# One core: the order of SyncE's loads in a chunked recurrent attention, and the pace of a background substitution

## The chip, the cores and the metric

The kernel runs on one core of a Trainium2 chip. The metric is the device time of that core in microseconds, the median of the runs. A core has five engines, each with its own queue that is worked in order: TensorE (PE in the rows; its weight loads are PEld), VectorE (DVE), ScalarE (ACT), GpSimd (POOL) and SyncE (SP), which here does nothing but issue transfers. Where an instruction at the head of a queue waits, everything behind it on that engine waits too.

## The reference

A recurrent attention over B = 4 batches, H = 8 heads, S = 768 tokens and D = 40, followed by two feed-forward layers.

```
for t in range(S):
    y[:, :, t] = einsum('bhd,bhde->bhe', r_t, state)
    Sa    = einsum('bhde,bhe->bhd', state, a_t)
    state = state * w_t[:, :, None, :] - einsum('bhd,bhe->bhde', Sa, b_t) + einsum('bhd,bhe->bhde', v_t, k_t)
x   = y as [B, S, H*D]
h   = relu(x @ w_in);  x2 = (h * sigmoid(conv3(h, conv_w))) @ w_out
u,v = halves of relu(x2 @ w_in2);  out = (u * (w_spatial @ normalized(v) + b_spatial)) @ w_out2
```

The change touches the attention alone.

## The kernel before

**Tiling.** The tokens are cut into 6 blocks n of 128 (two chunks of 64 each). A *unit* is one batch of one block with its 8 heads, so there are 24 units, kk = 4n + i. Two batches of a block are a *pair* p = kk // 2; their rows are loaded together. Within a chunk the recurrence is solved by a triangular system: a matrix is built from a and b (generator A), its 32x32 diagonal parts are inverted by a substitution (subst), the inverse is put together (Bp), applied along the chain of states (Cp), and the output y is formed (Dp).

**The loop.** Unit kk of the main loop interleaves, in 19 *parts* z = 0 to 18, the generators of several units by the string ORDER = "CDCBDCBCAAZAZBAZABZ": A of unit kk+9, Bp of unit kk+1, Cp of unit kk, Dp of kk (letter Z, its first four steps) and of kk-1 (letter D, its last two). So part 3 of a unit is the first step of Bp(kk+1): the matmuls pf (L226), which read DT; part 6 is its second: px (L238), which reads D1. Part 5 is pu of the second chunk (L290), which reads VM, made by VectorE behind part 2 (L303, L305). Parts 1 and 4 finish y of the unit before; part 4 ends with the product of py and ln on VectorE (L348). Part 9 is the first of A's transposes of P (L164), which reads P after VectorE's product P*il (L142, "pm", step 4 of an odd unit).

**What is issued when.** After each part, in this order: what is due by the counter of parts (`later(m, f)` puts f off by m parts, `tick` counts), then `pump` with so many steps of the background work as the rate gives (RATE steps a part from unit 3 on, RATE0 before), then the entries of SCHED and SCHEDC for this part. All of it is program order: every engine works its queue in just this sequence, SyncE too.

**SyncE's queue.** In an even unit SCHED[0] gives, for the pair po = kk // 2 + 5: il (2 transfers, L131), P (4, L112), araw (1, L100), lnA (1, L105). il is multiplied into P; G (L118, GpSimd, part 18) is araw times lnA, and AR (L123) its copy. The store of x (L350) is put off by 2 parts from part 4. `loadD` (L211, L213: DT, and D1 in two transfers) is put off by DTL parts from px of an odd Bp; it loads the inverse for the next pair into the only buffers of DT and D1, which must have been read: DT by pf and by copies into bdN (L232, VectorE and GpSimd), D1 by px. At part 18 the matrix is stored (tb, L178, 4 transfers). In an odd unit SyncE loads ln (part 5) and four transfers of Z and UR (L266, part 6).

**Substitution.** When both pairs of block n have passed through A (units 2, 6, 10, 14), the block's matrices are loaded (L, L186) in part 6 of the unit after, and SUB parts later subst(n) is put into the background list. For n >= 2 a step is VectorE's addition (L193) of one j and GpSimd's product tmp (L191) of the next, each reading what the other wrote; 30 of them and a last one in which GpSimd copies LT (L196). DDL parts after the last step the inverse is stored (dt, L198, and dd, L199); `loadD` reads it back from there.

Of the kernel before, what the change touches and what calls it, by code (L numbers as in the profile page):

```python
# [11 lines left out]
def attention(tc, keep, ident, r,k,v,w,a,b, x, spare=None):  # L12
# [3 lines left out]
    sy=nc.sync; V=nc.vector; T=nc.tensor; G_=nc.gpsimd; AC=nc.scalar  # L16
    with ExitStack() as ctx:
# [64 lines left out]
        def later(m,f):  # L82
            due.append((now[0]+m,f)); 
# [98 lines left out]
        def subst(n,ps=slice(0,128)):  # L182
            np_=ps.stop-ps.start
            if n not in Ls: Ls[n]=(sb.tile([128,HB,HB],F32,name="L"),sb.tile([128,HB*HB//4],F32,name="tmp"),sb.tile([128,HB,HB],F32,name="LT"))
            L,tmp,LT=(t[ps] for t in Ls[n])
            BQ[0].dma_start(out=L,in_=tb_d[n][ps])  # L186
            yield
            for j in range(1,HB-1):
                m=HB-1-j
                t=tmp[:,0:m*j].rearrange("p (m k) -> p m k",m=m)  # L190
                (G_ if n>=2 else V).tensor_tensor(t,L[:,j+1:HB,j:j+1].to_broadcast([np_,m,j]),L[:,j:j+1,0:j].to_broadcast([np_,m,j]),ALU.mult)  # L191
                yield
                V.tensor_tensor(L[:,j+1:HB,0:j],L[:,j+1:HB,0:j],t,ALU.add)  # L193
                if n<2: yield
            V.memset(L.rearrange("p t j -> p (t j)")[:,0:HB*HB:HB+1],1.0)
            (V if n==0 else G_).tensor_copy(LT,L.rearrange("p t j -> p j t"))  # L196
            def put():
                BQ[0].dma_start(out=dt_d[n][ps],in_=LT)  # L198
                BQ[0].dma_start(out=dd_d[n],in_=Ls[n][0][0:128:2])  # L199
                stored.update((n,j) for j in range(2) if ps.start<=j*64<ps.stop)  # L200
            later(DDL,put)
            yield
        inv={}; stored=set()
        def loadD(p):

            if p>=NK//2: return
            n,j=p//2,p%2
            assert (n,j) in stored,(p,stored,now,due)
            DT=sb.tile([128,H2,HB],F32,name="DT",bufs=1); D1=sb.tile([96,H2,HB],F32,name="D1",bufs=1)
            hs=slice(j*H2*4,(j+1)*H2*4)  # L210
            BQ[0].dma_start(out=DT,in_=dt_d[n][hs].rearrange("(b h q) t j -> (q t) (b h) j",b=2,q=4))  # L211
            for c in range(2):
                BQ[0].dma_start(out=D1[c*C:c*C+HB],in_=dd_d[n][j*H2*2:(j+1)*H2*2].rearrange("(b h q) t j -> q t (b h) j",b=2,q=2)[c])  # L213
            inv[n,j]=(DT,D1)
        def Bp(kk):

            i,n=units[kk]
            u=st[kk]; G=pair[n,i//2]['G']; h0=(i%2)*H
            DT,D1=inv[n,i//2]
            N=bdN[0]  # L220
            F=sb.tile([96,H,HB],F32,name="F",bufs=1)
            pf=ps.tile([128,H,HB],F32,tag="ps",name="pf")
            for h in range(H):
                for c in range(2):
                    lo=slice(c*C,c*C+HB); hi=slice(c*C+HB,c*C+C)
                    T.matmul(pf[lo,h],lhsT=G[hi,h0+h,0:HB],rhs=DT[hi,h0+h],start=True,stop=True)  # L226
            for c in range(2):
                lo=slice(c*C,c*C+HB)
                AC.copy(F[lo],pf[lo])
            for q in range(4):  # L230
                qs=slice(q*HB,(q+1)*HB)
                (G_.tensor_copy if q%2 else V.tensor_copy)(N[qs,:,q*HB:(q+1)*HB],DT[qs,h0:h0+H])  # L232
            yield
            px=ps.tile([128,H,HB],F32,tag="ps",name="px")
            for h in range(H):
                for c in range(2):
                    lo=slice(c*C,c*C+HB)
                    T.matmul(px[lo,h],lhsT=D1[lo,h0+h],rhs=F[lo,h],start=True,stop=True)  # L238
            for c in range(2):
                lo=slice(c*C,c*C+HB)  # L240
                AC.copy(N[lo,:,c*C+HB:c*C+C],px[lo])
            if i%2==1: later(DTL,lambda: loadD(kk//2+1))
            yield
            WT=u['WT']=[]
            for g in range(2):
                W=sb.tile([104,4,128],F32,name="WT",bufs=4); WT.append(W)
                p=ps.tile([128,4,128],F32,tag="ps",name="pw")
                for j in range(4):
                    T.matmul(p[:104,j],lhsT=G[:,h0+g*4+j,C:],rhs=N[:,g*4+j],start=True,stop=True)  # L249
                AC.mul(W,p[:104],-1.0)  # L250
                yield
# [55 lines left out]
        def Dp(kk):  # L307

            i,n=units[kk]
            pr=pair[n,i//2]; P=pr['P']; UR=pr['UR']; VM=st.pop(kk)['VM']; h0=(i%2)*H; bs=slice(i//2*2,i//2*2+2)  # L310
            s0=n*128
            ln,y=pr['ln'],pr['y']
            py=None
            ZVs,bdRs,SSs={},{},{}
            for part,g in ("z0","z1","S0","S1","y0","y1"):
                g=int(g)
                if part=="z":

                    ZV=ZVs[g]=sb.tile([80,4,168],F32,name="ZV",bufs=2)
                    bdR=bdRs[g]=sb.tile([80,4,2,C],F32,name="bdR",bufs=2)  # L320
                    p=ps.tile([128,4,2,C],F32,tag="ps",name="pz")
                    for j in range(4):
                        T.transpose(p[:80,j].rearrange("p c t -> p (c t)"),UR[:,h0+g*4+j].rearrange("p c e -> p (c e)"),ident)
                    AC.copy(ZV[:,:,0:C],p[:80,:,0])
                    for c in range(2):
                        AC.activation(bdR[:,:,c],p[:80,:,1],AF.Copy,scale=mB[:,c:c+1])
                    p=ps.tile([128,4,104],F32,tag="ps",name="pv")
                    for j in range(4):
                        T.transpose(p[:80,j],VM[:,g*4+j].rearrange("p c d -> p (c d)"),ident[:104,:104])
                    AC.copy(ZV[:,:,C:],p[:80])  # L330
                elif part=="S":
                    ZV,bdR=ZVs[g],bdRs[g]
                    SS=SSs[g]=sb.tile([128,4,2,C],F32,name="SS",bufs=2)
                    p=ps.tile([128,4,2,C],F32,tag="ps",name="pS")
                    for j in range(4):
                        T.matmul(p[:,j].rearrange("p c t -> p (c t)"),lhsT=ZV[:,j,0:2*C],rhs=bdR[:,j].rearrange("p c t -> p (c t)"),start=True,stop=True)  # L336
                    V.tensor_tensor(SS.rearrange("p h c t -> p (h c) t"),p.rearrange("p h c t -> p (h c) t"),mS.unsqueeze(1).to_broadcast([128,8,C]),ALU.mult)  # L337
                else:
                    ZV,bdR,SS=ZVs[g],bdRs[g],SSs[g]
                    if py is None: py=ps.tile([128,H,D],F32,tag="ps",name="py")  # L340
                    for j in range(4):
                        h=g*4+j
                        for c in range(2):
                            T.matmul(py[c*C:(c+1)*C,h],lhsT=SS[:,j,c],rhs=P[:,h0+h,c],start=True,stop=False)  # L344
                        for c in range(2):
                            T.matmul(py[c*C:(c+1)*C,h],lhsT=bdR[:,j,c],rhs=ZV[:,j,2*C:],start=False,stop=True)  # L346
                    if g==1:
                        V.tensor_tensor(y[:,h0:h0+H],py,ln[:,h0:h0+H],ALU.mult)  # L348
                        if i%2==1:
                            later(2,lambda: (AC if kk==NK-1 else sy).dma_start(out=x[bs,s0:s0+128].rearrange("b t f -> t b f"),in_=y.rearrange("p (b h) e -> p b (h e)",b=2)))  # L350
                yield

        units=[(i,n) for n in range(NU) for i in range(B)]
        NK=len(units)
# [17 lines left out]
        with tc.manual_schedule(engines={mybir.EngineType.SP,mybir.EngineType.DVE}):  # L372
            flat=lambda t: t.rearrange("p h e -> p (h e)")[:,0:512]
            def both(g,f):

                for _ in g:
                    yield
                    next(f,None)
            def steps(g,m):
                for _ in range(m): next(g,None)  # L380
# [22 lines left out]
            s0=subst(0); next(s0)  # L403
# [7 lines left out]
            s0=both(s0,chain((0 for _ in range(OFF)),l4))  # L411
            at=0
            for z in range(2):
                g=A(4+z); steps(g,3)
# [28 lines left out]
            with tc.manual_schedule():  # L443
# [9 lines left out]
                for kk in range(NK):  # L453
                    i,n=units[kk]
# [6 lines left out]
                    for g in ORDER if kk<TAIL else ORDER2:  # L461
# [5 lines left out]
                        while done<ex(kk-1)+(ex(kk)-ex(kk-1))*(z+1)//19:  # L467
                            next(later_layer,None); done+=1
                        tick(); acc+=RATE0 if kk<3 else RATE; pump(int(acc)); acc-=int(acc)
                        for s,f in SCHED[(kk+LA+1)%2]+SCHEDC[kk%2]:  # L470
                            if s==z:
# [21 lines left out]
OFF=24  # L493
L4N=21
L4T=15
RATE=0.65
RATE0=1.4
SCHED=[[[1, "il"], [5, "P"], [6, "araw"], [7, "ln"], [18, "g"], [18, "ar"]], [[1, "dup"], [4, "pm"]]]
SCHEDC=[[[2, "V"], [6, "Z"]], [[5, "Y"], [6, "Z"], [10, "V"]]]
SUB=4  # L500
TBL=3
LL2=7
LL=7
DDL=5
DTL=7
PMV=1
WARM0=3
WARM1=2
# [506 lines left out]
```

## Time and profile before

| | us |
|---|---|
| median of 3 runs (1005.5 to 1006.63) | 1005.76 |
| the profiled execution | 1006.02 |
| its span, first to last instruction | 1004.3 |
| TensorE busy | 861.1 (86%) |
| VectorE busy | 644.9 (64%) |
| ScalarE busy | 501.1 (50%) |
| GpSimd busy | 294.2 (29%) |
| mean granted TensorE clock | 0.895 |

The attention takes the span up to about 530 us, the loop over the units from about 123 us; the layers take the rest. Busy time of TensorE is counted at the clock that was granted: a stretch at half clock is busy and slow at once, so the share of busy time hides what a wait costs behind it. A unit of the loop is read best from the start of its pf. Where a row ends in brackets, these are the idle time of the engine just before and what ended it.

### The profile page before, as it was taken

The numbers are of one execution on the slowest core, as the hardware profiler recorded it, in microseconds if no ns is written. First come the engines' busy times: TensorE is split into PE (matmuls) and PEld (weight loads), VectorE is DVE, ScalarE is ACT, GpSimd is POOL, SyncE is SP. The second block draws the span as 40 slices with busy tenths as digits, with TensorE's granted clock in tenths as the row PEclk, the third lists the DMA queues.
The fourth block names the chain that finished last, engine by engine and source line by source line (L and its number), as shares of the span: only waits on it lengthen the run. The fifth ranks groups of instructions, "written<-read, shape, count | busy, mean of one in ns | idle before, by whom it ended". The sixth has DMA issues, their size and how long they took to land. (4 is left out here: it accounts for less than half of the span.)

```text
span 1004.3 us, 22325 instructions
## 1 busy us (share of the span) xinstructions
PE 861.1 (86%) x8923; PEld 806.9 (80%) x8923; DVE 644.9 (64%) x1412; ACT 501.1 (50%) x1115; POOL 294.2 (29%) x413
## 2 busy tenths in 40 slices
PE   0528579799989889979979789998999989998997
PEld 0326479788879889879868679998999979998897
DVE  6399688365464465577576997548763787258841
ACT  0423346456456555546765565346542665256531
POOL 1112021263262362453330001224412342234311
PEclk9965588798789789767978989999999999999999
DMA  7999898975785683646441132111000110011001
GB/s 131 199 192 189 153 191 126 161 111 106 130 132 111 104 133 86 148 76 147 101 125 56 64 93 75 38 47 54 1 24 20 52 42 24 21 40 31 10 1 44
DMA packets 292065, 90.04 MB, mean 90 GB/s; under 512 B 270960, under 2 KB 285040, under 8 KB 290800
## 3 DMA queue, kind: packets, MB, share of 16 engines
q1 hardware_dynamic: 291680, 88.20, 44.0%
q8 instruction: 72, 1.18, 0.5%
q14 instruction: 41, 0.34, 0.1%
q10 hardware_dynamic: 272, 0.33, 0.1%
HBM read 64.91 MB, written 23.59 MB: 88 GB/s over the span
## 5 line engine op out<-in xcount | busy, mean ns | idle before, releaser
L665 PE MATMUL psp<-spt,vv 128*128 128x384 f32 x576 | 105.5, 338 | 0.5 <-DVE vv L793 0.3
L665 PE MATMUL ph<-XT,G 128*128 128x386 f32 x512 | 103.2, 348 | 0.9 <-DVE XT L698 0.9
L665 PEld LDWEIGHTS psp<-spt,vv 128*128 128x128 f32 x576 | 100.2, 188 | 2.2 <-ACT vv L790 1.0
L193 DVE TENSOR_TENSOR L<-L,tmp 128x30 f32<-128x30 f32 (+9 forms) x180 | 67.1, 373 | 51.1 <-POOL tmp L191 49.1
L665 PEld LDWEIGHTS ph<-XT,G 128*128 128x128 f32 x512 | 94.4, 195 | 1.5 <-DVE XT L698 1.1
L727 POOL TENSOR_TENSOR gl<-c,gh 128x384 fp32r<-128x384 f32 x48 | 66.2, 1378 | 89.8 <-ACT gh L725 75.4
L191 POOL TENSOR_TENSOR tmp<-L 128x30 f32<-128x30 f32 (+14 forms) x120 | 60.7, 506 | 96.8 <-DVE L L193 81.1
L741 PE MATMUL acc<-gh,G 128*128 128x384 f32 x320 | 71.7, 350 | 16.0 <-ACT gh L725 9.9
L741 PEld LDWEIGHTS acc<-gh,G 128*128 128x128 f32 x320 | 56.5, 192 | 24.9 <-ACT gh L725 14.1
L344 PE MATMUL py<-P,SS 128*64 128x40 f32 x768 | 55.9, 248 | 9.4 <-DVE SS L337 9.4
L810 DVE TENSOR_TENSOR psp<-psp,bb 128x384 f32<-128x384 f32 x32 | 18.1, 566 | 70.6 <-PE psp L665 70.5
L171 PE MATMUL p<-PT,bdA 80*128 80x128 f32 x384 | 57.1, 302 | 5.7 <-ACT PT L165 5.6
L723 DVE TENSOR_TENSOR c<-h,c 128x384 f32<-128x384 f32 x64 | 39.3, 614 | 33.2 <-ACT c L720 32.9
L171 PEld LDWEIGHTS p<-PT,bdA 80*128 80x128 f32 x384 | 52.4, 215 | 8.5 <-ACT PT L165 8.5
L725 ACT CAST gh<-c 128x384 fp32r<-128x384 f32 x64 | 32.9, 514 | 52.7 <-DVE c L723 51.3
L815 POOL TENSOR_TENSOR zl<-u,zh 128x384 fp32r<-128x384 f32 x28 | 28.6, 1020 | 101.0 <-ACT zh L814 89.8
L172 DVE TENSOR_TENSOR G<-p,mT 128x512 f32<-128x512 f32 x48 | 32.8, 688 | 38.9 <-PE p L171 38.3
L346 PE MATMUL py<-ZV,bdR 80*64 80x40 f32 x768 | 55.6, 247 | 0.0
L249 PE MATMUL pw<-bdN,G 128*104 128x128 f32 x384 | 52.1, 281 | 4.1 <-issue 4.1
L336 PE MATMUL pS<-bdR,ZV 80*128 80x128 f32 x384 | 52.7, 282 | 2.2 <-ACT ZV L330 2.2
L344 PEld LDWEIGHTS py<-P,SS 128*64 128x64 f32 x768 | 44.7, 156 | 11.3 <-DVE SS L337 10.3
L292 ACT COPY ZU<-pu 64x160 f32<-64x160 f32 x96 | 27.5, 286 | 51.1 <-PE pu L290 49.0
(170 smaller groups left out, 2149.4 us busy)
## 6 DMA issues: line engine op xcount, KB each, us to landing
lq<-in_w_dram SPq DMA_DIRECT2D x12, 320.0 KB, 6.0
araw<-in_a_dram SPq DMA_DIRECT2D x12, 320.0 KB, 5.3
lam<-lm SPq DMA_DIRECT2D x12, 320.0 KB, 4.4
P<-in_b_dram SPq DMA_DIRECT2D x24, 160.0 KB, 4.5
P<-in_k_dram SPq DMA_DIRECT2D x24, 160.0 KB, 4.4
ilam<-lq SPq DMA_DIRECT2D x12, 320.0 KB, 4.8
lnA<-lam SPq DMA_DIRECT2D x12, 320.0 KB, 6.3
il<-ilam SPq DMA_DIRECT2D x24, 160.0 KB, 4.6
```

The source lines that it names most:

```text
L171: T.matmul(p3[:,j],lhsT=bdA[:,g*4+j].rearrange("p c t -> p (c t)"),rhs=PTs[g][:,j],start=True,stop=True)
L191: (G_ if n>=2 else V).tensor_tensor(t,L[:,j+1:HB,j:j+1].to_broadcast([np_,m,j]),L[:,j:j+1,0:j].to_broadcast([np_,m,j]),ALU.mult)
L193: V.tensor_tensor(L[:,j+1:HB,0:j],L[:,j+1:HB,0:j],t,ALU.add)
L249: T.matmul(p[:104,j],lhsT=G[:,h0+g*4+j,C:],rhs=N[:,g*4+j],start=True,stop=True)
L336: T.matmul(p[:,j].rearrange("p c t -> p (c t)"),lhsT=ZV[:,j,0:2*C],rhs=bdR[:,j].rearrange("p c t -> p (c t)"),start=True,stop=True)
L344: T.matmul(py[c*C:(c+1)*C,h],lhsT=SS[:,j,c],rhs=P[:,h0+h,c],start=True,stop=False)
L346: T.matmul(py[c*C:(c+1)*C,h],lhsT=bdR[:,j,c],rhs=ZV[:,j,2*C:],start=False,stop=True)
L665: L.tc.nc.tensor.matmul(out,lhsT=l,rhs=r,start=start and i==0,stop=stop and i==len(prs)-1)
L723: V.tensor_tensor(c,h[:,1:TH+1],c,ALU.mult)
L725: AC.copy(gh,c)
L727: def low(v): v.tensor_tensor(gl,c,gh.bitcast(F32),ALU.subtract)
L741: nc.tensor.matmul(acc[m],lhsT=l,rhs=r,start=f==0 and z<5 and z in (0,1,3),stop=f==NF-1 and z>=5)
```

## The change

Five constants, one schedule and two calls. `loadD` goes from 7 parts behind px to 1, which is the same part (for Bp(3) 5). araw and lnA of an even unit go from parts 6 and 7 to 2 and 3, P from part 5 to part 8. The store of x goes from 2 parts behind part 4 to 6 (the last one stays). RATE goes from 0.65 to 0.75 steps a part, SUB from 4 to 6, DDL from 5 to 3.

```diff
-            if i%2==1: later(DTL,lambda: loadD(kk//2+1))
+            if i%2==1: later(DTL if kk!=3 else DTL3,lambda: loadD(kk//2+1))
...
-                            later(2,lambda: (AC if kk==NK-1 else sy).dma_start(out=x[bs,s0:s0+128].rearrange("b t f -> t b f"),in_=y.rearrange("p (b h) e -> p b (h e)",b=2)))
+                            later(6 if kk<NK-1 else 2,lambda: (AC if kk==NK-1 else sy).dma_start(out=x[bs,s0:s0+128].rearrange("b t f -> t b f"),in_=y.rearrange("p (b h) e -> p b (h e)",b=2)))
...
-RATE=0.65
+RATE=0.75
 RATE0=1.4
-SCHED=[[[1, "il"], [5, "P"], [6, "araw"], [7, "ln"], [18, "g"], [18, "ar"]], [[1, "dup"], [4, "pm"]]]
+SCHED=[[[1, "il"], [2, "araw"], [3, "ln"], [8, "P"], [18, "g"], [18, "ar"]], [[1, "dup"], [4, "pm"]]]
...
-SUB=4
+SUB=6
...
-DDL=5
-DTL=7
+DDL=3
+DTL=1
+DTL3=5
```

## Rows read from the trace of the kernel before

**Rows 1.** Waits of TensorE, 119 to 512 us: total, times, longest

```profile
PE pf L226 <- DMA DT<-dt: 17.7, 7, 5.1
```

**Rows 2.** Timeline of TensorE, pf only: start us, length us

```profile
166.76 0.69 PE L226 MATMUL pf<-DT,G 32*32 32x32 f32 x32
186.49 1.07 PE L226 MATMUL pf<-DT,G 32*32 32x32 f32 x32 [5.14 <-DMA DT<-dt]
204.74 0.69 PE L226 MATMUL pf<-DT,G 32*32 32x32 f32 x32
221.12 0.69 PE L226 MATMUL pf<-DT,G 32*32 32x32 f32 x32 [2.09 <-DMA DT<-dt]
241.00 0.69 PE L226 MATMUL pf<-DT,G 32*32 32x32 f32 x32
258.32 1.06 PE L226 MATMUL pf<-DT,G 32*32 32x32 f32 x32 [2.46 <-DMA DT<-dt]
276.49 0.69 PE L226 MATMUL pf<-DT,G 32*32 32x32 f32 x32
...
313.33 0.69 PE L226 MATMUL pf<-DT,G 32*32 32x32 f32 x32
330.23 1.06 PE L226 MATMUL pf<-DT,G 32*32 32x32 f32 x32 [2.62 <-DMA DT<-dt]
348.29 0.69 PE L226 MATMUL pf<-DT,G 32*32 32x32 f32 x32
```

**Rows 3.** Windows of unit 7: busy us by engine, granted clock, DMA share, GB/s

```profile
258.30:268.00 9.70, 9.68 (x151) 9.08 (x152) 4.03 (x8) 4.48 (x12) 3.82 (x9) 0.51 0.89 161
268.00:276.50 8.50, 8.50 (x125) 8.33 (x123) 4.01 (x9) 5.07 (x14) 2.02 (x5) 1.00 0.45 62
```

**Rows 4.** Timeline of SyncE's queue, units 2 and 6

```profile
178.26 1.38 SPq L198 DMA_DIRECT2D dt<-LT  x1
...
182.63 0.36 SPq L211 DMA_DIRECT2D DT<-dt  x1
...
244.90 0.62 SPq L112 DMA_DIRECT2D P<-in_b_dram  x1
...
249.29 0.80 SPq L100 DMA_DIRECT2D araw<-in_a_dram  x1
...
252.30 2.49 SPq L211 DMA_DIRECT2D DT<-dt  x1
...
256.80 2.06 SPq L178 DMA_DIRECT2D tb<-G  x4
```

**Rows 5.** Timeline of TensorE, px of unit 6

```profile
243.75 0.69 PE L238 MATMUL px<-F,D 32*32 32x32 f32 x32
```

**Rows 6.** Timeline of GpSimd, LT of block 1 and units 4 to 5

```profile
170.97 1.98 POOL L196 COPY LT<-L 128x1024 f32<-128x1024 f32 x1 [0.46 <-DVE L L195]
...
212.98 0.61 POOL L191 TENSOR_TENSOR tmp<-L 128x234 f32<-128x234 f32 x1 [0.51 <-DVE L L193]
214.11 0.62 POOL L191 TENSOR_TENSOR tmp<-L 128x238 f32<-128x238 f32 x1 [0.52 <-DVE L L193]
...
219.71 1.53 POOL L118 TENSOR_TENSOR G<-araw,lnA 128x640 f32<-128x640 f32 x1
```

**Rows 7.** Timeline of VectorE, unit 5

```profile
219.79 1.72 DVE L193 TENSOR_TENSOR L<-L,tmp 128x234 f32<-128x234 f32 x1 [0.71 <-POOL tmp L191]
...
222.06 0.49 DVE L305 TENSOR_TENSOR VM<-m,lamC 40x320 f32<-40x320 f32 x1
...
226.41 1.80 DVE L142 TENSOR_TENSOR P<-P,il 128x1280 f32<-128x1280 f32 x1
```

**Rows 8.** Waits of VectorE, 204.7 to 241 us

```profile
DVE L L193 <- POOL tmp L191: 9.3, 13, 1.7
DVE G L172 <- PE p L171: 1.7, 2, 1.5
```

**Rows 9.** The page's DMA issues: transfers, KB each, median us to landing

```profile
P<-in_k_dram SPq DMA_DIRECT2D x24, 160.0 KB, 4.4
```

## The prediction

> **What bounds the kernel now.** I read the waits of TensorE first, for the loop over the 24 units only (119 to 512 us). Its largest entry is the matmul pf waiting for the transfer of DT: 17.7 us in seven waits [rows 1]. The timeline of pf then shows which units these are [rows 2]: those with a wait lie in odd units. The DT that an even unit u loads serves units u+2 and u+3, and the pf of u+2 runs in the odd unit u+1, so that a late DT is felt there first. The rows of three even units, to the next pf and with its wait subtracted, give the length of a unit that nothing disturbs: 166.76 to 186.49 less 5.14 is 14.59 us, 241.00 to 258.32 less 2.46 is 14.86, 313.33 to 330.23 less 2.62 is 14.28; the mean is 14.6. The unit that follows each wait is longer though it has no wait for DT in it: 186.49 to 204.74 is 18.25, 258.32 to 276.49 is 18.17, 330.23 to 348.29 is 18.06. The windows over unit 7 say why: after the wait at 258.32 the granted clock is 0.51 (the 1.2 GHz level) over 9.7 us in which TensorE is busy throughout, then 1.00 (2.4 GHz) again [rows 3]. So one late DT costs its wait and some 3.6 us of slow clock behind it.
>
> Why DT is late is read in SyncE's timeline of unit 6 [rows 4]. Behind the store of x come four transfers of P from 244.90 on, then araw at 249.29, lnA, and DT only at 252.30; D1 follows, and the stores of tb at 256.80. But px, the last reader of the old D1, ran at 243.75 and took 0.69 [rows 5]: from 244.44 on DT could have gone. It stood 7.9 us behind issues that nobody needed as urgently.
>
> **The change, part by part.** The sum is made against the profiled execution, 1006.0 us (span 1004.3, and 1.7 around it); the median of the runs is 1005.8, so the two are one for this purpose, and the forecast is counted from 1005.8.
>
> *DT behind px (7 parts after px becomes 1), araw and lnA at parts 2 and 3, P at part 8, x at part 9.* SyncE's order in an even unit becomes il, araw, lnA, DT, D1, P, x, tb. Nothing is added: each issue is moved past others of the same queue. In unit 6, DT goes at about 244.5 and needs between 3.9 us (182.63 to 186.49, the issue and the pf that had waited for it [rows 2, 4]) and 6.0 us (252.30 to 258.32): it is there by 248.4 to 250.5. pf wants it at 258.32 - 2.46 = 255.86. At least 5 us of cover. Units 6 and 10 so lose their waits, 2.46 and 2.62, and the slow unit behind each, 18.17 - 14.6 = 3.6 and 18.06 - 14.6 = 3.5: **6.1 us each**.
>
> What is late next there? P. DT and D1 took SyncE 4.5 us (252.30 to 256.80), so the four P go from 249.0 and take 4.4 (244.90 to 249.29 [rows 4]), to 253.4; the last, issued about 0.7 before that, lands 4.4 later [rows 9], near 257.1. The product P*il on VectorE (1.8 us [rows 7]) is read by TensorE in part 9: pf to px is 2.75 us (241.00 to 243.75) and three parts more are 2.3 (14.6 us over 19 parts, 0.77 each), 5.1 behind pf, so it must begin by 255.86 + 5.1 - 1.8 = 259.2. Cover 2 us; I cost it at nothing, and name it as a rival below. araw and lnA go earlier into time in which SyncE stood waiting for x, and cost nothing; GpSimd's product G then has its data earlier. x is stored 4 parts later; its buffer is next written two units on, cost nothing.
>
> *Unit 2* is different: the inverse of block 1 is only just finished. GpSimd's transposing copy LT runs from 170.97 for 1.98, to 172.95 [rows 6]; the store dt went at 178.26, behind x, P, araw and lnA, and DT at 182.63, 4.4 us later, since it reads what dt wrote [rows 4]. In the new order (DDL 3 and DTL3 5) dt comes in part 8 ahead of P and SyncE waits there for LT: dt and dd at 173.0 to 174.0, P to 178 (3.5 to 4.4 us), x, and DT at 178.0 to 179.0, when dt has landed. pf is served 3.9 to 5 us later, 181.9 to 184; it wants DT at 186.49 - 5.14 = 181.35. Of the 5.14 some 1.2 stay (bounds 0.5 and 2.7). Whether the clock holds over so short a wait no row decides: between 0 and 3.6 us I take half. **5.7 us** (2.4 to 8.2).
>
> *Unit 0* waits 17.7 - 5.14 - 2.46 - 2.62 less three waits near 2.3 in units 4, 8 and 12, about **0.6 us**, and no more: its VectorE is full of the substitution of block 1, whose rate 1.4 is not touched.
>
> *Units 4, 8, 12 and 16, the pairs in which a block is substituted.* Here the DT wait goes as well, but another stands directly behind it. In unit 5 VM, which pu in part 5 reads, is finished by VectorE at 222.06 + 0.49 = 222.55; pf stood at 221.12 after a wait of 2.09 [rows 2], so without it at 219.03, and pu lies between pf and px, within 2.75 us of pf. Ahead of VM in VectorE's queue lies a substitution step of 1.72 us beside GpSimd's G, which began at 219.71 [rows 6, 7]. So 0.8 us or more of the 2.09 is taken back at once. Over the whole pair (204.7 to 241.0) VectorE waits 9.3 us for GpSimd's half of a step and only 1.7 for TensorE [rows 8]: VectorE with GpSimd is the bound of these pairs, and TensorE's waits are a consequence. Now RATE. A step in the middle of a block takes 214.11 - 212.98 = 1.13 us [rows 6]. With 0.77 us a part, 0.65 steps a part ask for a step every 1.18 us, 0.75 for one every 1.02. Before, the two engines just kept pace; after, they don't. By counting the steps from the rates, 13 instead of 11 or 12 large steps lie between pf of unit 4 and VM of unit 5, and 3 instead of 2 before P*il. Bounds for a pair: three steps more in front of TensorE, 3.4 us lost; or the DT wait (2.3) and the slow unit (3.6) both gained, 5.9 us. Nearest is the row of VectorE's waits, which leaves 1.7 us to be won, against up to 3.4 from the pace, while the block ends 5 parts earlier and gives some of it back. I take **1 us lost in each of the four pairs, 4 in all**. SUB 4 to 6 starts a block two parts later, when its rows have landed; they delayed GpSimd and not TensorE, cost nothing.
>
> What the rows show of two engines together: VectorE's half of the step at 219.79 took 1.72 us while G ran its 1.53 beside it, where a whole step, both halves, is 1.13 [rows 6, 7]. The Trainium skill (SBUF — State Buffer, Who interferes with whom) says that a VectorE instruction with two SBUF inputs and a GpSimd instruction that reads SBUF take one port pair in turn, the second blocked for the whole of the first. By that rule the denser steps would cost more than their own length, since VM's product and P*il have two SBUF inputs too: an estimate by it is two more steps of 0.6 us on GpSimd met by VectorE in each of four pairs, 5 us, and the sum would be 996; by the rows above it is 991.
>
> **Sum:** 6.1 + 6.1 + 5.7 + 0.6 - 4 = 14.5 us; 1005.8 - 14.5 = **991 us**.
>
> **The rivals.** (a) *Substitution becomes the bound: slower.* Place: VectorE's queue in units 4, 8, 12 and 16. Each such pair loses not 1 but 3.4 us and a further slow-clock unit of 3.6, 7 in all: 24 us more, 1015. It decides where a step (1.13) is longer than its spacing (1.02); against it, the steps at both ends of a block are shorter and the block still has 30. Chance 0.11. (b) *P behind DT lands too late.* If SyncE's issues are slower than in unit 6 by more than the 2 us of cover, TensorE stands in part 9 and the clock falls again: 1.5 + 3.6 in units 6 and 10, 10 us more, 1001. For it: the issues in rows 4 differ, 0.62 for a P and 2.49 for DT, so their sum can. Chance 0.09. (c) *The clock does not stay up*, since other waits (pu for VM, P for il) remain and pull it down all the same: the 3.6, 3.5 and 1.8 are not won, 1000. Against it: the even units of rows 2 keep to 14.3 to 14.9 us though VM and SS lie on their path too. Chance 0.08. (d) *The substitution pairs are freed too*, since a TensorE at full clock frees buffers earlier and VectorE's waits shrink: 5.9 won instead of 1 lost in units 4, 8 and 12, 20.7 us more, 970. Against it: the 1.7 us of slack. Chance 0.17. That the change doesn't do what it says is little to be feared, since the queue is issued in program order.
>
> **How the numbers follow.** Forecast 0.55, (d) 0.17, (a) 0.11, (b) 0.09, (c) 0.08. The forecast's own bounds are unit 2 (3 us either way) and the four pairs (2.4 us each way at most): 980 to 1002. The range reaches into (d), as partial freeing lies between 991 and 970, and takes in (b) and (c): 975 to 1003; (a) and the far half of (d) are left out. A measurement of this kernel can tell about 0.2%, 2 us. Faster: the forecast, (c), (d) and most of (b), 0.85; same 0.05; slower 0.10.
>
> **What would show it.** Right: pf's wait for DT all but gone (below 3 us in the loop, what is left in unit 3); DT issued right behind px, some 8 us earlier in the unit; the slow stretch after pf gone in units 7 and 11, and these two pairs near 29 instead of 35 us; the pairs of units 4, 8, 12 still 35 to 39 us with waits for VM, SS or P. Wrong: a wait for P in units 7 and 11; VectorE's wait for GpSimd much above before with pairs over 40 us (a); all pairs near 30 us (d); slow clock without a wait ahead of it (c).

## The result and the profile after

| | before | after |
|---|---|---|
| median, us | 1006.19 (1005.5 to 1008.22, 4 runs) | 992.55 (989.23 to 994.93, 4 runs) |
| profiled execution, us | 1006.02 | 990.97 |
| its span, us | 1004.3 | 989.3 |
| mean granted TensorE clock | 0.895 | 0.904 |

The ratio of after to before is 0.9859 (95% interval 0.9823 to 0.9894): 13.6 us faster in the medians. Here and below a run over 1.5% above the fastest of its kernel is left out of the ratio, but not of the median and the range beside it; only the pace alone (two runs in each of its sets) and the last kernel (one run) have such runs, so that the ratios of the pace alone lean towards faster. The forecast was 991, in the range 975 to 1003.

Waits of TensorE in the kernel after, 119 to 512 us (total, times, longest). pf's wait for DT, the 17.7 us of [rows 1], is down to one; the waits for VM and SS, made by VectorE, now lead the list.

```profile
PE pu L290 <- DVE VM L305: 14.2, 8, 2.8
PE py L344 <- DVE SS L337: 9.8, 7, 3.8
PE pz L323 <- POOL ZU L294: 4.8, 5, 1.9
PE p L164 <- DVE P L142: 4.6, 3, 1.5
PE pw L249 <- issue: 4.2, 1, 4.2
PE pf L226 <- DMA DT<-dt: 3.1, 1, 3.1
```

Timeline of TensorE after, pf only, units 2 to 12 (compare [rows 2]).

```profile
165.59 0.69 PE L226 MATMUL pf<-DT,G 32*32 32x32 f32 x32
183.25 0.69 PE L226 MATMUL pf<-DT,G 32*32 32x32 f32 x32 [3.08 <-DMA DT<-dt]
200.34 0.69 PE L226 MATMUL pf<-DT,G 32*32 32x32 f32 x32
215.13 0.69 PE L226 MATMUL pf<-DT,G 32*32 32x32 f32 x32
237.32 0.69 PE L226 MATMUL pf<-DT,G 32*32 32x32 f32 x32
251.53 0.69 PE L226 MATMUL pf<-DT,G 32*32 32x32 f32 x32
265.74 0.69 PE L226 MATMUL pf<-DT,G 32*32 32x32 f32 x32
...
304.00 0.69 PE L226 MATMUL pf<-DT,G 32*32 32x32 f32 x32
318.21 0.69 PE L226 MATMUL pf<-DT,G 32*32 32x32 f32 x32
332.65 0.69 PE L226 MATMUL pf<-DT,G 32*32 32x32 f32 x32
```

Units 6 and 7 take 14.21 us each, to the hundredth, where before unit 7 alone took 18.17. From such rows the pairs, pf to pf:

| pair of units | before, us | after, us | difference | what it holds |
|---|---|---|---|---|
| 2 | 37.98 | 34.75 | -3.2 | dt of block 1 just finished |
| 4 | 36.26 | 36.98 | +0.7 | substitution of block 2 |
| 6 | 35.49 | 28.42 | -7.1 | none |
| 8 | 36.84 | 38.26 | +1.4 | substitution of block 3 |
| 10 | 34.96 | 28.65 | -6.3 | none |
| 12 | 36.25 | 38.02 | +1.8 | substitution of block 4 |
| 14 | 27.30 | 27.08 | -0.2 | none, no loads any more |
| 16 | 39.40 | 38.44 | -1.0 | substitution of block 5, weights of the layers |
| 18 | 27.34 | 26.31 | -1.0 | none |

With 0.1 in pair 0 and 1.0 by which the loop begins earlier (the part ahead of it is not touched, and when the same kernel was run again, f0_whole below, the loop began 2.5 us later than in the kernel before) this is 16.1 us at unit 20; the layers give 1.1 us back, and the span is 15.0 shorter.

SyncE's queue after, unit 6 (compare [rows 4]); px of that unit ran from 239.47 to 240.16. DT is issued at 240.98, when lnA has left the queue, 3.66 us after pf instead of 11.30, with araw and lnA ahead and P and x behind.

```profile
237.15 2.30 SPq L100 DMA_DIRECT2D araw<-in_a_dram  x1
239.50 1.31 SPq L105 DMA_DIRECT2D lnA<-lam  x1
240.98 2.44 SPq L211 DMA_DIRECT2D DT<-dt  x1
243.53 1.78 SPq L213 DMA_DIRECT2D D<-dd  x2
245.36 0.92 SPq L112 DMA_DIRECT2D P<-in_b_dram  x1
...
248.91 1.96 SPq L350 DMA_DIRECT2D x<-ln  x1
```

Windows over unit 7 and over the stretch behind pu of unit 5 after (busy us by engine with counts, granted clock, DMA share, GB/s; compare [rows 3]): unit 7 runs at the 2.4 GHz level (1.00) from end to end; near the 1.2 GHz level (0.51) TensorE is in the pair with a substitution, behind the wait for VM.

```profile
251.53:265.74 14.21, 14.21 (x274) 13.78 (x272) 8.93 (x18) 9.89 (x25) 5.43 (x12) 1.00 1.03 177
...
219.73:229.00 9.27, 7.73 (x90) 6.92 (x91) 6.00 (x12) 4.54 (x11) 6.45 (x12) 0.51 0.59 80
```

### The profile page after: what moved, and what is told of

The parts are those of the page before. It is cut to its first block, busy times and chain, and to the rows that moved or that the text cites. A ratio compares the mean times of both kernels' runs of the same rounds, so it can differ in the third digit from the quotient of the medians.

```text
span 989.3 us, 22329 instructions
## 1 busy us (share of the span) xinstructions
PE 853.4 (86%) x8923; PEld 799.2 (81%) x8923; DVE 640.6 (65%) x1412; ACT 501.2 (51%) x1115; POOL 293.5 (30%) x413
## 3 DMA queue, kind: packets, MB, share of 16 engines
q8 instruction: 72, 1.18, 0.5%
## 5 line engine op out<-in xcount | busy, mean ns | idle before, releaser
L193 DVE TENSOR_TENSOR L<-L,tmp 128x30 f32<-128x30 f32 (+9 forms) x180 | 69.1, 384 | 54.7 <-POOL tmp L191 52.1
L344 PE MATMUL py<-P,SS 128*64 128x40 f32 x768 | 53.7, 243 | 10.2 <-DVE SS L337 10.2
L346 PE MATMUL py<-ZV,bdR 80*64 80x40 f32 x768 | 53.2, 242 | 0.0
```

## The experiments

The times of runs on the same chip vary more than those of the kernel before on record: it ran from 1001.4 to 1012.5 beside the first four. So a verdict below rests on the length of pairs in a trace where a few microseconds decide, and on medians with their ratio to before otherwise.

**The order alone, the pace alone.** The change holds two things that were forecast with opposite signs; each was run without the other.

```
e1_order_only: the change, but RATE=0.65  SUB=4  DDL=5
e2_pace_only:  before, but RATE=0.75  SUB=6  DDL=3
```

> The changed order of SyncE's queue with the old pace (0.65 steps a part, SUB 4, DDL 5). My theory: the gain comes from the order alone, about 18 us in units 2, 3, 6, 7, 10 and 11, and the pace costs 1 to 2 us in each of the four pairs with a substitution. So this should be 4 us faster than the whole change, near 988, with the pairs of units 4, 8, 12 at 35 to 36.5 us and those of units 6 and 10 still under 30. Rival: the pace is what brings dt and DT in time for units 6 and 10; then the wait of pf for DT returns there and the time is near 1000.

Measured: 988.53 us (987.2 to 988.92), ratio 0.9812 (0.9766 to 0.9858). Pairs 6 and 10 take 28.99 and 28.47 us, pairs 4, 8 and 12 take 36.59, 36.71 and 36.18. The whole change, run again later (f0_whole below), has 991.47. So the order carries all of the gain, and the faster pace takes 0.4 to 1.8 us of it back in each of these three pairs. dt was in time for units 7 and 11 without it. In unit 3 pf waits 1.66 us here and 3.08 in the whole change: with DDL 5 P is issued ahead of dt, from 167.12 on, while SyncE would stand; with DDL 3 it comes between dt and DT.

> The old order with the new pace (0.75 steps a part, SUB 6, DDL 3). My theory: pf's waits for DT stay as before (17 to 18 us in the loop) and the four pairs with a substitution get 1 to 2 us longer: 1006 to 1014, not faster than before. Rival: a part of the gain comes from the pace, by an earlier dt; then 995 to 1003 and pf's wait in unit 7 and 11 smaller.

Measured: 1002.13 us (992.43 to 1009.86, 10 runs), ratio 0.9939 (0.9902 to 0.9977). The time missed what was expected: some 4 us faster than before, not 0 to 8 slower. The runs spread over 17 us, and the trace is of the longest, 1009.86: pairs 4, 8, 12 and 16 take 37.26, 36.92, 38.20 and 40.70 in it, 4.3 us more than before in sum, as expected, and pf waits 14.8 us for DT. What the shorter runs gained this trace can't show, so the kernel was run again.

> The pace alone (old order, 0.75 steps a part, SUB 6, DDL 3) once more, since its first runs spread from 992 to 1010 us and its trace was of the longest. My theory: it gains nothing in the pairs with a substitution (36.9 to 38.5 us, 1 more than before) and its shorter runs come from pf's waits for DT falling to 1.3 us or so, after which the clock sometimes holds; then the trace of a run near 1000 shows a unit 7 or 11 of about 14.2 us behind a wait. Rival: the gain lies in the pairs with a substitution; then they are at or below 36 us and units 7 and 11 still at 18.

Measured: 1006.29 us (993.18 to 1010.15, 10 runs), ratio 0.9968 (0.9931 to 1.0004), its profiled execution 1007.84. Timeline of TensorE, pf of units 6 to 8 and 10 to 12:

```profile
240.24 0.69 PE L226 MATMUL pf<-DT,G 32*32 32x32 f32 x32
256.63 0.69 PE L226 MATMUL pf<-DT,G 32*32 32x32 f32 x32 [2.11 <-DMA DT<-dt]
273.84 0.69 PE L226 MATMUL pf<-DT,G 32*32 32x32 f32 x32
...
311.25 0.69 PE L226 MATMUL pf<-DT,G 32*32 32x32 f32 x32
326.56 0.69 PE L226 MATMUL pf<-DT,G 32*32 32x32 f32 x32 [1.03 <-DMA DT<-dt]
345.28 0.69 PE L226 MATMUL pf<-DT,G 32*32 32x32 f32 x32
```

Pairs 4, 8, 12 and 16 take 36.99, 37.41, 37.62 and 40.55: 0.7, 0.6, 1.4 and 1.2 us more than before, 3.8 in sum. So the second trace gives the same cost of the pace, about 1 us a pair, as the first. Against it stand pairs 6 and 10 with 33.60 and 34.03, 1.9 and 0.9 us less than before. In pair 10 DT is waited for less long (1.03, before 2.62); in pair 6 the wait gives only 0.35 (2.11, before 2.46), and why both its units are shorter beyond that no row says. The slow units behind (17.21 and 18.72) stay. The trace is again of a long run, so that where the shorter ones gain stays open; the first trace has a unit 11 of 14.21 behind a wait of 1.34, as was expected of a short run, but it is of a long one too. Over both sets of runs the pace alone gains nothing that they agree on: one interval lies below 1 by 0.2% and the other holds 1. The whole 13.6 us need the order.

**P one part earlier.** This goes at the one term of the sum that was badly sized, unit 2.

```diff
-SCHED=[[[1, "il"], [2, "araw"], [3, "ln"], [8, "P"], ...
+SCHED=[[[1, "il"], [2, "araw"], [3, "ln"], [7, "P"], ...
```

> The whole change with P one part earlier, in part 7: behind DT in every even unit but unit 2, where it now goes ahead of dt. In the changed kernel SyncE waits there for LT of block 1 with P behind dt, and pf of unit 3 waits 3.1 us. My theory: the issue time of P, 4.7 us, is what makes DT of unit 3 late; that wait goes to zero with the slow clock behind it, 3.1 + 3.5 us: 6 to 7 us faster than the whole change, near 986. Rival: dt must land before DT is issued, so DT can't come earlier than LT + 4.4 + 3.9 us; then at least half of the wait stays and the gain is 0 to 2 us.

Measured: 986.07 us (983.6 to 989.19), ratio 0.9788 (0.9736 to 0.984). SyncE's queue in unit 2 of the whole change: SyncE stands from 165.74 to 171.82 with nothing to issue, because the store dt at its head waits for LT, and then P takes 4.9 us between dt and DT.

```profile
164.17 1.57 SPq L105 DMA_DIRECT2D lnA<-lam  x1
171.82 0.34 SPq L198 DMA_DIRECT2D dt<-LT  x1
...
172.84 0.62 SPq L112 DMA_DIRECT2D P<-in_b_dram  x1
...
177.72 0.66 SPq L350 DMA_DIRECT2D x<-ln  x1
178.48 0.41 SPq L211 DMA_DIRECT2D DT<-dt  x1
```

With P in part 7 the same queue, and the wait of DT at its head:

```profile
174.57 0.88 SPq L112 DMA_DIRECT2D P<-in_k_dram  x1
176.57 0.34 SPq L198 DMA_DIRECT2D dt<-LT  x1
...
177.56 0.73 SPq L350 DMA_DIRECT2D x<-ln  x1
181.47 0.37 SPq L211 DMA_DIRECT2D DT<-dt  x1
...
SPq L211 <- DMA dt<-LT: 3.1, 1, 3.1
```

And pf with P in part 7 (timeline of TensorE, units 2 to 4): the wait is 0.32 instead of 3.08, and the unit behind it takes 14.21 instead of 17.09.

```profile
170.66 0.69 PE L226 MATMUL pf<-DT,G 32*32 32x32 f32 x32
185.26 0.69 PE L226 MATMUL pf<-DT,G 32*32 32x32 f32 x32 [0.32 <-DMA DT<-dt]
199.47 0.69 PE L226 MATMUL pf<-DT,G 32*32 32x32 f32 x32
```

Pair 2 takes 28.81 us against 34.75: 5.9 us from one digit, about the gain expected. But the theory had only a part of it right. Without P between them DT still goes 4.90 us behind dt, against 6.66 with it, and SyncE stands 3.1 of these waiting for dt to land: that is the rival's floor. Of the 2.76 us by which the wait shrank, 1.8 came from there and 1.0 from DT being served sooner after its issue (3.79 us to pf, 4.77 in the whole change). Behind the 0.32 that was left the clock held, which gave another 2.9, and that was partly luck: in the three later kernels with P in part 7 pf waits 0.90 to 1.28 us, the clock falls, and the pair takes 33.1 to 33.4.

**GpSimd's G earlier.** Is it the place of G beside the chain that makes VM late, or the chain itself?

```diff
-... [18, "g"], [18, "ar"]]
+... [13, "g"], [13, "ar"]]
```

> The whole change with GpSimd's G and AR in part 13 of an even unit instead of part 18. In the changed kernel pu of units 5, 9 and 13 waits 2.8 us for VM, behind a substitution step that ran beside G. My theory: VectorE and GpSimd together are the bound of these pairs, so the 3.4 us of G and AR only move; the wait for VM shrinks and waits for SS or P take its place, pairs of 36 to 38.5 us, time within 4 us of the whole change. Rival: the place of G is what makes VM late; then the wait goes, with the slow clock behind it, 5 us a pair in three pairs, near 977.

Measured: 992.14 us (988.9 to 995.13), ratio 0.9851 (0.9798 to 0.9904). Pairs 4, 8 and 12 take 35.91, 38.14 and 37.12. The waits of TensorE in this kernel, 119 to 512 us:

```profile
PE py L344 <- DVE SS L337: 17.9, 10, 4.6
PE pu L290 <- DVE VM L305: 9.5, 11, 2.1
```

VM went from 14.2 to 9.5 and SS from 9.8 to 17.9: the wait changed its name. The rival asked for 5 us a pair; the three pairs are 1.1, 0.1 and 0.9 us shorter than in the first trace of the change, and the time is the same. As expected, and against the rival; that the 3.4 us of G and AR on GpSimd cost the chain the same wherever they stand is what this suggests, not a row.

**The whole change again, beside the next three.** 

> The whole change once more, on the chip and in the rounds of the runs beside it, as their measure: 988 to 995, pairs of units 4, 8 and 12 of 37 to 38.5 us, pf of unit 3 waiting 3 us.

Measured: 991.47 us (990.42 to 998.24), ratio 0.9882 (0.9836 to 0.9928); pairs 4, 8 and 12 of 37.42, 36.96 and 37.94, pf of unit 3 waiting 3.26 us.

**Both single gains together.** The order with P in part 7 and RATE=0.65, SUB=4, DDL=5.

> The changed order with P in part 7 and the old pace (0.65, SUB 4, DDL 5): both single gains together. My theory: they lie in different units (order with P at 7 in unit 3, the pace in units 4 to 17) and add: 2 to 4 us faster than P at 7 alone and 1 to 3 faster than the order alone with P at 8, whose pf in unit 3 waited 1.7 us: 982 to 986. Rival: with the old pace dt of block 1 goes in part 10 behind P and x, DT behind it, and the wait of unit 3 comes back: no faster than either, 986 to 989.

Measured: 985.94 us (979.22 to 991.21), ratio 0.9782 (0.9737 to 0.9828): not faster than P at 7 alone, so the gains did not add. The trace sides with the rival. pf of unit 3 waits 1.14 us and the unit behind it takes 17.23 again; pairs 4, 8 and 12 have the 36.69, 36.75 and 36.19 us of the old pace. With DDL 5 the store dt came behind P and x, but that is 0.25 us only (172.61, where LT ended at 172.36); most of the wait is dt's landing, since DT went 5.27 us behind dt, against 4.90 with P in part 7 and the faster pace.

**Is the slow clock a consequence of the wait?** In the kernel before, TensorE was given idle work while it waited in units 7 and 11.

```diff
                         z+=1
+                        if z==3 and kk in (7,11): warm(ident,18)
```

> The kernel before with 18 matmuls of ident on ident in front of pf in units 7 and 11 only, nothing else changed: TensorE is busy while it waits for DT (2.5 us there), DT comes no earlier. My theory: the half clock behind these waits follows from TensorE standing idle; filled, units 7 and 11 keep the full clock and pf to the next pf falls from 18.2 to about 14.6 us in both, 7 us in all, near 999. Rival: the clock falls there for another reason (what runs behind pf); then pf to pf stays at 18 us and the time does not change.

Measured: 1000.45 us (996.53 to 1003.69), ratio 0.9954 (0.9914 to 0.9994), 4.9 us less than before in the medians, for doing more work. Timeline of TensorE, pf and the filling matmuls, units 6 to 8:

```profile
238.74 0.69 PE L226 MATMUL pf<-DT,G 32*32 32x32 f32 x32
...
253.51 4.29 PE L371 MATMUL warm<-ident 128*128 128x128 f32 x36
257.73 0.69 PE L226 MATMUL pf<-DT,G 32*32 32x32 f32 x32
271.94 0.69 PE L226 MATMUL pf<-DT,G 32*32 32x32 f32 x32
```

The filling took 4.2 us, 1.7 more than the wait, so unit 6 came to 18.99 us instead of 17.32. But unit 7 came to 14.21 instead of 18.17, and unit 11 to 14.21 instead of 18.06, with the same DT, no earlier than before (issued 11.29 us behind pf in unit 6, before 11.30). So the 3.9 us behind such a wait (3.6 against an undisturbed unit) are the price of TensorE standing idle: this is shown, not argued. The net of 4.6 us over the two pairs agrees with the 4.9 in the medians. The trace itself is of the shortest run, 996.53, and half of its distance to before lies outside these two pairs.

**Is the hand-over between two engines the bound of the substitution?**

```diff
-(G_ if n>=2 else V).tensor_tensor(t, ...
+V.tensor_tensor(t, ...
```

on top of the order, P in part 7, RATE=0.65, SUB=4, DDL=5.

> The changed order with P in part 7 and the old pace, and the substitution's product tmp of blocks 2 to 5 on VectorE instead of GpSimd, so that a step no longer passes between two engines. My theory: the pairs with a substitution are bound by the hand-over, 1.13 us a step of which VectorE works 0.4; with both halves on VectorE a step is 0.75 to 0.8, the waits for VM and P shrink and the pairs of units 4, 8 and 12 come to 31 to 34 us, 972 to 980. Rival: VectorE's own work is the bound; each step then adds 0.35 us to it and the pairs stay at 36 us or get longer, 984 to 995.

Measured: 981.19 us (978.58 to 984.05), ratio 0.9749 (0.9714 to 0.9783). Timeline of VectorE: a step is now 0.86 us from tmp to tmp (205.87 to 206.73), against 1.13 in [rows 6], with no gap in it.

```profile
205.87 0.40 DVE L191 TENSOR_TENSOR tmp<-L 128x228 f32<-128x228 f32 x1
206.30 0.40 DVE L193 TENSOR_TENSOR L<-L,tmp 128x228 f32<-128x228 f32 x1
206.73 0.40 DVE L191 TENSOR_TENSOR tmp<-L 128x234 f32<-128x234 f32 x1
```

Pairs 4, 8 and 12 take 34.80, 35.34 and 33.69: 1.4 to 2.5 us less than with GpSimd, not the 2 to 5 expected. The window over unit 4 says why. Its columns are the length and the busy times of TensorE, its weight loads, VectorE, ScalarE and GpSimd; VectorE is busy 14.23 of 15.00 us.

```profile
198.00:213.00 15.00, 15.00 (x299) 14.52 (x297) 14.23 (x30) 10.82 (x25) 4.42 (x7) 1.00 0.58 106
```

So the hand-over was part of the bound, and once it is gone VectorE's own work is near to being it. Theory and rival each had a part.

**dt ahead of x in that kernel.** The last one with DDL=3.

> The order with P in part 7, pace 0.65, SUB 4, tmp on VectorE, and DDL 3 of the change instead of 5: the store dt of block 1 comes in part 8 of unit 2, ahead of the store of x, not behind it in part 10. With DDL 5 pf of unit 3 waited 1.1 to 1.3 us and the unit behind it took 17.2 us. My theory: the wait goes below 0.5 us and unit 3 falls to 14.2 us: 4 us faster than tmp on VectorE with DDL 5, 976 to 979. Rival: dt waits for LT anyway and nothing moves, 980 to 983.

Measured: 985.63 us (981.44 to 992.23), ratio 0.9792 (0.9749 to 0.9836). The rival's mechanism held, though the time missed both ranges: dt went at 173.30, when LT ended (173.27). DT was issued 5.35 us behind dt (173.30 and 178.65) though only dd and x stood between them, since it reads what dt wrote; pf of unit 3 still waited 0.90 us and the unit behind it took 17.27. The landing of dt is the floor that is left there. The trace is of the longest run, 992.23, and unit 8 takes 18.63 us in it, behind a wait of 1.30 for VM, against 14.38 without DDL 3; whether DDL 3 causes that was not tested.

**A slower pace.** RATE=0.60, SUB=4, DDL=2 and P in part 6, tmp on GpSimd.

> The order with P in part 6 and a slower pace, 0.60 steps a part (SUB 4, DDL 2), tmp on GpSimd as before. A step every 1.28 us is asked for where a large one takes 1.13. My theory: VectorE keeps up, the waits for VM and SS in units 5, 9 and 13 shrink, the last steps fall into units 6 and 10, which have room: pairs of units 4, 8, 12 of 34 to 36 us against 36.2 to 36.7 at 0.65 and 37 to 38.3 at 0.75, time 981 to 985. Rival: the length of these pairs comes from G and AR beside the chain and not from the pace; then they stay at 36 to 37 us and the steps in units 6 and 10 cost more, 985 to 992.

Measured: 980.74 us (978.23 to 984.18), ratio 0.9769 (0.9731 to 0.9807). Pairs 4, 8 and 12 take 34.28, 35.65 and 35.39; pairs 6 and 10, which now hold the last steps, 28.97 and 29.87; pair 2 takes 29.35, since pf of unit 3 waits only 0.56 us and the clock holds behind it. With 0.65 (36.2 to 36.7) and 0.75 (37.0 to 38.3) the order is 0.60, 0.65, 0.75 in all three pairs. P's part moved with it, but between parts 8 and 7 at 0.65 these pairs differ by 0.1 at most.

**Slower pace and tmp on VectorE.** The last two together.

> Both together: order with P in part 6, tmp on VectorE, pace 0.60, SUB 4, DDL 2. My theory: VectorE is full in the pairs with a substitution at 0.65 (busy 14.2 of 15 us); with fewer steps in them they come to 32 to 34 us and the tail lies in units 6 and 10 without a wait: 972 to 977. Rival: dt then comes too late for DT in units 6 and 10, whose pf waits again: 978 to 985.

Measured: 985.24 us (981.34 to 1018.05), ratio 0.9789 (0.9737 to 0.9841): no gain over either. pf waits for DT nowhere in the loop, against the rival, and pair 4 is the shortest of all kernels, 33.40. But pair 8 takes 35.96, with a unit 8 of 16.58, and pair 12 takes 34.96 where tmp on VectorE alone had 33.69. VM and SS lead the waits of TensorE as before, 12.0 and 8.0 us. So what these two parts win may be the same few microseconds of VectorE's queue, not won twice. The trace also reaches pf of unit 2 4.4 us later than that of the slower pace alone (170.82 against 166.40), ahead of any instruction in which the two kernels differ. Why the median is not below 981 is not settled.

The two best, the slower pace with GpSimd (980.74) and tmp on VectorE (981.19), both beat the change by some 11 us; their ranges overlap.

## Why the prediction was right, point by point

**The total: right in its main cause, closer than its terms.** Against the 14.5 us of the sum the span is 15.0 us shorter. Units 6 and 10 gave 1.2 more than forecast, the pairs with a substitution cost 1.0 less, units 0 and 2 gave 2.9 less. What the sum had no term for brought 1.2 net: 1.0 by which the loop began earlier, 1.3 in pairs 14 and 18, 1.1 lost in the layers. That these all but cancel is luck; that the order carries the gain is not.

**DT behind px: right.** Units 6 and 10 were forecast at 6.1 us each, and measured 7.1 and 6.3. In unit 6 DT went 3.7 us behind pf and pf of unit 7 did not wait. Of the 7.1, 2.46 is the wait, 3.96 the clock (18.17 to 14.21), the rest unit 6 itself: an undisturbed unit takes 14.21, not the 14.6 taken from three even units. That the clock would stay up was the weakest link of this step; the filled kernel shows it as cause and consequence.

**P behind DT costs nothing: right.** In units 7 and 11 TensorE never waited for P. The last P of unit 6 was issued at 247.92 + 0.89 and pf of unit 7 stood at 251.53. Rival (b) did not occur.

**Unit 2: direction right, size wrong.** The step that failed is "of the 5.14 some 1.2 stay (bounds 0.5 and 2.7)". 3.08 stayed, outside the bounds, and the clock fell for a whole unit (17.09), where half was taken: 3.2 us won instead of 5.7. DT was issued at 178.48, inside the forecast 178.0 to 179.0, but only because everything stood 1.2 us earlier than in the trace before: pf of unit 2, the end of LT (171.79, the row below), and the time at which pf of unit 3 wanted DT, 183.25 - 3.08 = 180.17 and not 181.35.

```profile
169.80 1.99 POOL L196 COPY LT<-L 128x1024 f32<-128x1024 f32 x1 [0.47 <-DVE L L195]
```

Counted from the end of LT, pf wants DT 8.4 us later, as forecast. What was mis-sized is the way from LT to DT: 6.69 us, where the forecast has 5.05 to 6.05. P took 4.9 us of it, more than the 3.5 to 4.4 that the forecast gave it. From DT to pf it was 4.77, inside its bounds of 3.9 to 5. The run with P in part 7 shows that P was the part that could be won, and that the landing of dt, 4.9 us from issue to issue, lay close under it. The sign "below 3 us" for pf's wait was missed by 0.08.

**Pairs with a substitution: right in kind and nearly in size.** 1 us lost in each of four was forecast; measured were 0.7, 1.4, 1.8 and -1.0, in sum 2.9 of 4. VectorE after, unit 5 (compare [rows 7]): VM is done at 219.10 + 0.49, and pu waits 2.85 us for it, more than the 2.09 that pf had waited for DT.

```profile
216.84 1.70 DVE L193 TENSOR_TENSOR L<-L,tmp 128x220 f32<-128x220 f32 x1 [0.69 <-POOL tmp L191]
...
219.10 0.49 DVE L305 TENSOR_TENSOR VM<-m,lamC 40x320 f32<-40x320 f32 x1
```

The order alone settles which part did this: its four pairs take 148.9 us in sum, before 148.8. So the lost wait for DT of 2.1 to 2.4 us gave nothing there, as the forecast had it, and the loss is the pace's. Pair 16 went the other way by 1.0, and with the pace too, as the order alone has 39.44 in it; it holds the layers' weights on VectorE as well, and why the pace helps there no run shows.

**The pace, 1.13 us a step against 1.02 and 1.18 between two: right.** The three paces order the three pairs as the spacing says. Rival (a) needed 7 us a pair and had 1.3 on average in the three. Rival (d) was that these pairs are freed as TensorE gets faster; they are not, and what frees them, by 1 to 2.5 us, is fewer steps in them or no hand-over.

**The port rule.** Beside G VectorE's half of a step took 1.70 us after (216.84, above), as 1.72 before, and 0.40 without G (206.30, with both halves on VectorE); G's row after:

```profile
216.76 1.53 POOL L118 TENSOR_TENSOR G<-araw,lnA 128x640 f32<-128x640 f32 x1
```

VectorE's instruction ends 0.25 us behind G. The Trainium skill's rule (SBUF — State Buffer, Who interferes with whom), that such a pair of instructions takes a port pair in turn, agrees with these rows. The further 5 us that were estimated from it, for 996, did not come: the pairs lost 2.9 in all, so the price that was estimated from the rule was too high; how often the denser steps met was not counted.

**Unit 0:** 0.6 forecast, 0.1 measured. Its wait of 0.69 for DT is gone and 2.94 for SS stands in its place (before, two of 0.83 and 1.68), so nothing came of it.

**The bounds.** The bounds named for unit 2 and the four pairs add up to 12.6 us each way, 978 to 1004, not 980 to 1002; the range does not hang on it. That a measurement of this kernel can tell 2 us was too bold: the kernel before ran from 1001.4 to 1012.5.

## What to carry to other kernels

Read a wait of TensorE together with the unit behind it: here the waits of 2.5 and 5.1 us for DT were each followed by a unit some 3.6 us longer at the lower clock level, and where a wait was removed (units 7 and 11) both came back. In a queue that is issued in order, put the transfer that the next stage waits for directly behind the instruction that frees its buffer, and put whatever can go early ahead of the first entry that must wait, not behind it; what is read back from DRAM then still waits for its store to land (4.9 us here). Background work that hands over between two engines wants wider spacing than one step with its hand-over, in the stretch where its steps are longest: here, of the three spacings tried for a step of 1.13 us, 1.28 had the shortest pairs and 1.02 the longest.

## What the hardware showed beside that

Whether TensorE's clock falls behind a wait is not a matter of the wait's length alone. In unit 3, waits of 0.90, 1.14, 1.28, 1.66, 2.98, 3.08 and 3.26 us (g1, f1, f3, e1, e4, after, f0) were followed by units of 17.1 to 18.7 us, and waits of 0.32 and 0.56 (e3, h1) by 14.21; the length behind the wait hardly depends on the wait. But in unit 11 of the pace alone, one and the same program, a wait of 1.34 was followed by 14.21 in one trace and a wait of 1.03 by 18.72 in the other. So a wait's price is nearly all or nothing, 2.9 to 4.5 us or none, and it can differ from run to run. The pf ahead of the loop, near 112 us, shows the same. It waits 4.5 to 5.5 us for DT in all fourteen traces, and the stretch behind it takes 15.5 to 16.6 us in ten and 19.3 to 19.8 in four. The whole change has one of each kind (16.31 and 19.32), and so has the pace alone (15.74 and 19.56); by pf of unit 2 the slower trace is 2.4 and 4.8 us behind. In the whole change the granted clock over 112.0 to 128.0 is 0.66 in one and 0.50 in the other. A few such places would make runs of one kernel lie some 5 to 10 us apart, as they did here; whether they are the whole reason was not tested.
